# Retention and two feed-forward layers on one core: when weight preparations are split, when the first plain tile starts, and when the last activated values are stored

## The chip, the cores and the metric

The kernel runs on one core of one Trainium2 chip. The metric is the device time of one execution in microseconds. The core's engines are named as in the profile: PE (matrix products; PEld is its weight load), DVE (vector engine), ACT (scalar engine), POOL (GpSimd) and SP, which here only issues transfers. ACT issues transfers too; such a row is marked ACTq, one of SP is marked SPq. Each engine carries out its own instructions in order.

## What is computed

Four batches of eight heads go through a linear retention over 768 positions; the result, 3072 rows of 512, goes through two feed-forward layers of width 2048.

```python
state = gamma * state + k[t] outer v[t];  y[t] = scale * q[t] @ state     # per batch and head
x = y as 3072 x 512
h = x @ w_in;  g = maximum(0.01 * h, h);              x = g @ w_out       # first layer
h = x @ w_in2; g = h * (1 / (1 + exp(-1.702 * h)));   out = g @ w_out2    # second layer
```

The weights come as 64-bit floats. The chip makes 32-bit floats of them by integer steps on their two words.

## The kernel before

**Products.** Every operand of a product in the feed-forward layers is split into a rounded part ("hi", a copy on ACT) and the rest ("lo", a subtraction on DVE); three products of the parts stand for one. `split` (L153 and L150) is this pair of instructions.

**Phases.** First comes the retention in 24 steps of 128 positions (`retention`), and among its steps the 16 tiles of the first layer's `x @ w_in` for the first 512 rows. Then come the other five blocks of 512 rows, 16 tiles each (`ffn_in`): 12 matmuls of 128x512 into one of six PSUM banks, one activation on ACT that evicts it (L243), and one store that ACT issues (L245). These are the "plain" tiles. The three products that follow, first `w_out` (`Second`), second `w_in` (`First`), second `w_out` (`Second` again), use a scheme of seven block products in place of eight, for which the weights' blocks are also added and subtracted. `First` works on 32 pairs of a row block and an eighth of the width.

**Conversions in the retention.** The 16 weight tiles of the plain product are loaded (`load_raw`), converted (`convert`: two steps on ACT, L171 and L172, four on DVE, L175 to L181, then `round_up`, L190) and split (`finish`, its lo part on POOL). `W0 = 4` sets the step at which the first plain tile stands; `work` is called from two steps earlier on. A step has the scores of the next position block (L278, and their masking on DVE, L281), the state update (L317 on DVE), the output products, and the scaling of the output on DVE (`put`, L330 or L342). The scores have one place in PSUM: those of step s+2 wait until L281 has read those of step s+1.

**Preparations.** 36 half slots of later weights are prepared beside the plain tiles of blocks 1 to 5, and 12 more in the third phase. `Prep.start` gives out the steps by a clock, `Later`, that ticks once per tile: load at once; at tick 3 `words` (L171, L172 on ACT, L175 to L181 on DVE) and `sums` (L190 and three L150 on DVE); for the first 6 preparations (they are kept in place) and the first 6 of the second `w_in` (numbers 16 to 21; they are stored in two parts) also at tick 3 a split of 896 columns; at tick 4 the store. A preparation is begun whenever `given < (n + 1) * 36 // 67` for tile n. Raw words and result have three places each; the split's hi part goes back to the place of the raw words.

**The end.** The last product is written by `last_result`, twice, for 128 of the output's columns each time: two copies of PSUM, one on ACT and one on DVE, a transpose on PE, two copies again, two stores.

## Time and profile before

| | |
|---|---|
| median of 3 runs | 1090.22 us (1087.55 to 1092.33) |
| the profiled execution's own time | 1088.18 us |
| its span, first to last instruction | 1086.1 us |
| PE busy | 1057.2 us, 97% |
| DVE busy | 814.3 us, 75% |
| ACT busy | 586.7 us, 54% |
| mean granted clock of PE | 0.995 |

PE is busy nearly throughout. The page cuts the span into 40 slices of 27 us: PE reads 9 tenths or more in 37 of them, 7 in the first, and 8 in that from 272 to 299 us and in the last. The granted clock reads 9 tenths or more in each. So the places where PE waits, or where its clock fell, have to be looked for one by one, in the views of waits, windows and timelines.

### The profile page before, as it was taken

The page shows a single profiled execution, that of the slowest core. Times are in us where ns is not written, and L with a number is a line of the kernel's source. Part 1 is how long each engine was busy: PE and PEld are TensorE (multiplying, and loading weights), DVE is VectorE, ACT ScalarE, POOL GpSimd, SP SyncE. Part 2 cuts the span into 40 slices and gives each one's busy share as a digit, 9 for nine tenths or more (in the row PEclk, how much of TensorE's full clock was granted, in tenths as well). Part 3 has the DMA queues.
Part 4 walks back from the last instruction along what each step waited for, and adds up shares of the span by engine and source line. Part 5 has one row for each costly group of instructions (what it writes and reads, how often), then busy time and mean ns, then how long its engine had stood idle before and what let it go on. Part 6 is the DMA issues. An engine that isn't in the chain of part 4 may idle for free.

```text
span 1086.1 us, 16941 instructions
## 1 busy us (share of the span) xinstructions
PE 1057.2 (97%) x6042; PEld 903.9 (83%) x6043; DVE 814.3 (75%) x1384; ACT 586.7 (54%) x1114; POOL 90.3 (8%) x88
## 2 busy tenths in 40 slices
PE   7999999999899999999999999999999999999998
PEld 5777887787678888888888999999999788888886
DVE  5987736786679598688789677686767996885883
ACT  5766534554455564544545666465565645555553
POOL 1211100000000000000000203444300000000000
PEclk9999999999899999999999999999999999999999
DMA  9899664797799613723529844858387535235322
GB/s 345 304 364 395 205 214 151 250 366 260 255 330 314 207 41 100 259 76 123 190 69 320 309 145 164 289 174 283 138 281 244 218 97 190 101 97 194 105 70 78
DMA packets 128164, 225.81 MB, mean 208 GB/s; under 512 B 11088, under 2 KB 72784, under 8 KB 124752
## 3 DMA queue, kind: packets, MB, share of 16 engines
q1 hardware_dynamic: 97440, 178.29, 48.0%
q10 hardware_dynamic: 30640, 46.45, 11.7%
q8 instruction: 47, 0.77, 0.3%
q14 instruction: 37, 0.30, 0.1%
HBM read 138.71 MB, written 85.98 MB: 207 GB/s over the span
## 4 chain that ended last, share of the span: by engine, by line
PE 74%; DVE 9%; DMA 7%; ACT 4%; issue 3%; POOL 1%; ACTq 1%; SPq 0%; DVEq 0%; POOLq 0%
PE psum L758 42%; PE psum L576 18%; PE psum L239 7%; DMA gd<-e 2%; PE psum L278 2%; ACT e L243 2%; DMA b<-w1o 1%; PE psum L308 1%; DVE b L150 1%; DVE b L181 1%; DVE b L190 1%; PE psum L982 1%; DMA c<-w1i 1%; DMA h<-qkv 1%; PE psum L301 1%
## 5 line engine op out<-in xcount | busy, mean ns | idle before, releaser
L758 PE MATMUL psum<-c,h 128*128 128x512 f32 x1008 | 228.8, 389 | 0.0
L758 PEld LDWEIGHTS psum<-c,h 128*128 128x128 f32 x1008 | 189.3, 188 | 39.2
L758 PE MATMUL psum<-e,h 128*128 128x512 f32 x768 | 182.0, 391 | 1.7 <-DVE e L150 1.7
L758 PEld LDWEIGHTS psum<-e,h 128*128 128x128 f32 x768 | 143.4, 188 | 31.9 <-DVE e L150 2.5
L239 PE MATMUL psum<-d,h 128*128 128x512 f32 x576 | 139.4, 398 | 8.4 <-ACT e L243 4.9
L239 PEld LDWEIGHTS psum<-d,h 128*128 128x128 f32 x576 | 107.5, 190 | 36.0 <-ACT e L243 6.9
L239 PE MATMUL psum<-a,h 128*128 128x512 f32 x576 | 133.6, 393 | 3.3 <-ACT e L243 3.1
L239 PEld LDWEIGHTS psum<-a,h 128*128 128x128 f32 x576 | 109.0, 190 | 27.4 <-ACT e L243 3.9
L576 PE MATMUL psum<-b,h 128*128 128x384 f32 x576 | 111.0, 335 | 2.0 <-ACT psum L642 2.0
L576 PE MATMUL psum<-c,h 128*128 128x384 f32 x576 | 110.2, 334 | 0.3 <-DVE d L607 0.3
L576 PEld LDWEIGHTS psum<-b,h 128*128 128x128 f32 x576 | 100.5, 188 | 3.8 <-ACT psum L642 3.5
L576 PEld LDWEIGHTS psum<-c,h 128*128 128x128 f32 x576 | 100.6, 188 | 0.9 <-DVE d L607 0.6
L715 ACT CAST c<-b 128x512 fp32r<-128x512 f32 x96 | 59.3, 622 | 57.1 <-DVE c L150 35.6
L150 DVE TENSOR_TENSOR c<-b,c 128x512 fp32r<-128x512 f32 x96 | 65.4, 689 | 18.8 <-ACT c L715 16.6
L590 ACT ACTIVATE d<-psum 128x384 f32<-128x384 f32 x96 | 47.1, 491 | 57.3 <-PE psum L576 48.9
L715 ACT CAST e<-a 128x512 fp32r<-128x512 f32 x77 | 47.2, 622 | 43.5 <-PE psum L758 15.0
L243 ACT ACTIVATE e<-psum 128x512 f32<-128x512 f32 x80 | 47.5, 593 | 42.4 <-PE psum L239 34.2
L150 DVE TENSOR_TENSOR e<-a,e 128x512 fp32r<-128x512 f32 x77 | 52.3, 688 | 22.1 <-ACT e L715 20.9
L150 DVE TENSOR_TENSOR h<-h 128x384 fp32r<-128x384 f32 (+2 forms) x80 | 44.7, 593 | 20.6 <-ACT h L153 11.5
L150 POOL TENSOR_TENSOR a<-a 128x768 f32<-128x768 f32 x7 | 13.2, 1892 | 485.8 <-DMA h<-wds 470.7
L594 DVE TENSOR_TENSOR d<-psum,d 128x384 f32<-128x384 f32 x96 | 51.2, 548 | 2.6 <-ACT d L590 2.1
L758 PE MATMUL psum<-f,h 128*128 128x512 f32 x192 | 49.0, 390 | 0.0
(139 smaller groups left out, 1464.6 us busy)
## 6 DMA issues: line engine op xcount, KB each, us to landing
gd<-d ACTq DMA_DIRECT2D x128, 192.0 KB, 2.7
h<-qkv SPq DMA_DIRECT2D x21, 1024.0 KB, 8.0
gd<-e ACTq DMA_DIRECT2D x80, 256.0 KB, 4.7
d<-gd SPq DMA_DIRECT2D x64, 256.0 KB, 4.1
b<-gd SPq DMA_DIRECT2D x64, 256.0 KB, 3.9
a<-gd SPq DMA_DIRECT2D x48, 256.0 KB, 4.6
c<-w1i SPq DMA_DIRECT2D x16, 512.0 KB, 8.1
xd<-e SPq DMA_DIRECT2D x12, 512.0 KB, 3.2
```

Of the source, the lines that this page charges most:

```text
L150: e.tensor_tensor(out=o, in0=x, in1=y, op=ALU.subtract)
L181: lambda f, high: nc.vector.scalar_tensor_tensor(out=f, in0=f, scalar=0x7FFFFFFF, in1=high, op0=ALU.bitwise_and, op1=ALU.bitwise_or))
L190: e.tensor_tensor(out=f.bitcast(I32), in0=f.bitcast(I32), in1=low.bitcast(I32), op=ALU.add)
L239: nc.tensor.matmul(out=h, lhsT=w[:, a, k], rhs=xs[blk % 2][k][:, c], start=(i == 0), stop=(i == 3 * NP - 1), skip_group_check=True)
L243: nc.scalar.activation(out=t, in_=h, func=AF.Lrelu)
L278: nc.tensor.matmul(out=ps[:, e, n], lhsT=kT[r, n], rhs=qT[r, n], start=True, stop=True, skip_group_check=True)
L301: nc.tensor.matmul(out=kv[r, n], lhsT=ks[:, 2 * n + e], rhs=v[:, n, r], start=(c == 0 and n == 0), stop=True, skip_group_check=True)
L576: nc.tensor.matmul(out=t, lhsT=w[:, k, a], rhs=x[:, b, k], start=(start and m == 0), stop=(m == 5), skip_group_check=True)
L590: nc.scalar.activation(out=s, in_=src, func=AF.Sigmoid, scale=1.702)
L594: nc.vector.tensor_tensor(out=dst, in0=src, in1=s, op=ALU.mult)
L715: nc.scalar.copy(out=t[:, 0], in_=self.block_of(*item))
L758: nc.tensor.matmul(out=t[:, j], lhsT=w[:, j, a], rhs=x[:, b], start=(new and q == 0 and m == 0), stop=(q == NQ - 1 and m == 2), skip_group ...
```

## The change

1. **Preparations.** The split stands at tick 4 in place of 3, the store at tick 6 in place of 4. The split's hi part has a ring of its own of two places, one of which is taken from the ring of evicted tiles: that one has six places in place of eight. Preparations are begun at a rate of 36 in 64 tiles in place of 67. In the third phase a preparation's steps begin with one empty step.
2. **Retention.** `W0` is 6 in place of 4. `work` is cut in two: load and conversion stand before the step's output products (`work_first`), the split of the tile before and the rounding after the step's outputs (`work_last`). The rounding of the first two tiles is done on POOL. The first two raw loads stand in steps 1 and 2 in place of step 0. ACT's first instruction works on another piece of memory than the one that PE's warm-up products read.
3. **Third phase's end.** Stores of activated values that come due in its last iteration are put on a list, and issued two at a time behind the first products of the last phase. That phase prepares four operands ahead in place of three.
4. **The end.** The two first copies of the last product are both on ACT; each half is transposed on its own, into another bank, and stored on its own.

```diff
-    W0 = 4
+    W0 = 6
-    def work(between=lambda: None):
-        n = done[0]
-        done[0] += 1
+    def work_first(n):
         if n + 2 < KF:
             load_raw(n + 2)
-        between()
         if n < KF:
             convert(n)
+    def work_last(n):
         if 0 < n <= KF:
             finish(n - 1)
         if n < KF:
-            round_up(*conv[n])
+            round_up(*conv[n], nc.gpsimd if n < 2 else nc.vector)
...
-        nc.scalar.copy(out=idle[:, :2], in_=idle[:, 2:4])
+        first = few.view(5, 8)
+        nc.gpsimd.memset(first, 0.0)
+        nc.scalar.copy(out=first[:, :4], in_=first[:, 4:])
...
+            n = None
+            if s >= W0 - 2 and done[0] < KF + 1 and (s <= W0 or now_in[s - 1]):
+                n = done[0]
+                done[0] += 1
+                work_first(n)
             o = a_out(s)
-            if s >= W0 - 2 and done[0] < KF + 1 and (s <= W0 or now_in[s - 1]):
-                work(lambda: a_store(s, o))
-            else:
-                a_store(s, o)
+            a_store(s, o)
+            if n is not None:
+                work_last(n)
...
-            if s == 0:
-                load_raw(0)
-                load_raw(1)
+            if s in (1, 2):
+                load_raw(s - 1)
...
-    g_ring = ring(run_of(Area("e"), 8, 2), TB)
+    g_area = Area("e")
+    g_ring = ring(run_of(g_area, 6, 2), TB)
...
-            self.hi = self.raw.bitcast(F32).rearrange("p b f t -> p (b f t)")[:, : 7 * P].rearrange("p (i f) -> p i f", i=7)
+            self.hi = next(self.rings[2])
...
-                clock.at(3, self.split if split else self.keep)
+                clock.at(4, self.split if split else self.keep)
             if not keep:
-                clock.at(4, self.store_split if split else self.store)
+                clock.at(6, self.store_split if split else self.store)
...
-            out = [lambda: words_scalar(self.f, self.low, raw[:, :, 1])]
+            out = [lambda: None, lambda: words_scalar(self.f, self.low, raw[:, :, 1])]
...
-            if given < min(N_IN1, (n + 1) * N_IN1 // 67):
+            if given < min(N_IN1, (n + 1) * N_IN1 // 64):
...
-                store = lambda t: nc.scalar.dma_start(out=self.dst[f * NQ + q][:, cols], in_=t)
+                def store(t):
+                    put = lambda: nc.scalar.dma_start(out=self.dst[f * NQ + q][:, cols], in_=t)
+                    if self.ending:
+                        self.pending.append(put)
+                    else:
+                        put()
...
+                self.ending = not now
...
-            second2.begin(later2, 0, NQ, 3, 14)
+            second2.begin(later2, 0, NQ, 4, 14)
...
     def done3(n, blk, i, q):
+        for _ in range(2):
+            if first2.pending:
+                first2.pending.pop(0)()
...
         for k in range(2):
-            copy[k](t[:, k * n : k * n + n], h[:, j, k * n : k * n + n])
-
-        def turn():
-            for b in range(4):
...
+            nc.scalar.copy(out=part(t, k), in_=part(h[:, j], k))
+
+        def turn(k):
+            for b in range(2):
...
+        for k in range(2):
+            later.at(1 + k, lambda k=k: turn(k))
+            later.at(2 + k, lambda k=k: store(k))
```

Three places show what this makes of the engines' order. In the rows, the names with a letter are areas of memory; the line numbers of the change are one or a few off those of before.

ACT in block 1, around the first preparation that is kept in place (the CAST of 128x896 is its split's hi part, L171 and L172 its words, or L172 and L173 in the change; the ACTIVATE of psum is a tile's eviction). Before:

```order
L171 ACTIVATE b<-b 128x512
L172 ACTIVATE b<-b 128x512
L153 CAST h_1599<-b 128x896
L243 ACTIVATE e<-psum 128x512
L245 DMA gd_77<-e 128x512
L243 ACTIVATE e<-psum 128x512
L245 DMA gd_77<-e 128x512
L171 ACTIVATE b<-b 128x512
```

The same place in the change:

```order
L172 ACTIVATE b<-b 128x512
L173 ACTIVATE b<-b 128x512
L242 ACTIVATE e<-psum 128x512
L244 DMA gd_77<-e 128x512
L154 CAST h_1617<-b 128x896
L242 ACTIVATE e<-psum 128x512
L244 DMA gd_77<-e 128x512
L172 ACTIVATE b<-b 128x512
```

One eviction and its store moved from behind the CAST to between the words and the CAST.

DVE in the retention, around the first conversion (the four instructions from TENSOR_SCALAR of c to SCALAR_TENSOR_TENSOR are its words, ISA its rounding, the TENSOR_TENSOR of 128x1024 the masking of the scores). Before, in steps 2 and 3:

```order
L317 TENSOR_TENSOR b<-psum,f 128x256
L330 TENSOR_TENSOR h_84<-psum,f 128x2x128
L330 TENSOR_TENSOR h_84<-psum,f 64x2x128 x2
L175 TENSOR_SCALAR c_184<-c_184 128x512
L177 TENSOR_SCALAR b<-b 128x512
L179 TENSOR_SCALAR b<-b 128x512
L181 SCALAR_TENSOR_TENSOR b<-b,c_184 128x512
L190 ISA b<-c_184,b 128x1024
L281 TENSOR_TENSOR b<-psum,b 128x1024
```

In the change, in steps 4 and 5:

```order
L280 TENSOR_TENSOR b<-psum,b 128x1024
L176 TENSOR_SCALAR c_233<-c_233 128x512
L178 TENSOR_SCALAR b<-b 128x512
L180 TENSOR_SCALAR b<-b 128x512
L182 SCALAR_TENSOR_TENSOR b<-b,c_233 128x512
L316 TENSOR_TENSOR b<-psum,f 128x256
L341 TENSOR_TENSOR h_84<-psum,f 128x2x2x128
L280 TENSOR_TENSOR b<-psum,b 128x1024
```

The words moved two steps back, and within the step from behind the state update and the output's scaling to ahead of them; the rounding is no longer on DVE here.

ACT at the end of the third phase (ACTIVATE of d from psum is that phase's activation, the CAST of 128x512 an operand of the last phase). Before:

```order
L590 ACTIVATE d<-d 128x384
L590 ACTIVATE d<-psum 128x384
L586 DMA gd_78<-d 128x384 x4
L715 CAST e<-a 128x512
L715 CAST f<-a 128x512
```

In the change:

```order
L601 ACTIVATE d<-d 128x384
L601 ACTIVATE d<-psum 128x384
L727 CAST f<-a 128x512
L592 DMA gd_78<-d 128x384 x2
L727 CAST e<-a 128x512
L592 DMA gd_78<-d 128x384 x2
```

The stores moved from ahead of the operands' casts to between them, and one more operand (e) is cast earlier, in the third phase.

## Rows read from the trace of the kernel before

**Rows 1.** The page's head and its part 1: busy time, share of the span, instructions.

```profile
span 1086.1 us, 16941 instructions
...
PE 1057.2 (97%) x6042; PEld 903.9 (83%) x6043; DVE 814.3 (75%) x1384; ACT 586.7 (54%) x1114; POOL 90.3 (8%) x88
```

**Rows 2.** Waits of PE over the whole span: us in total, times, longest us.

```profile
PE psum L278 <- DVE b L281: 4.3, 2, 3.9
...
PE psum L576 <- ACT psum L642: 2.0, 4, 0.7
...
PE psum L758 <- DVE e L150: 1.7, 1, 1.7
...
PE psum L278 <- DMA h<-qkv: 1.3, 2, 0.7
```

**Rows 3.** Waits of PE from 140 to 345 us, the plain tiles beside the preparations.

```profile
PE psum L239 <- ACT e L243: 7.5, 6, 2.9
...
PE psum L239 <- DVE d L150: 3.4, 2, 2.7
```

**Rows 4.** Windows: us, each engine's busy us (x instructions), granted clock, DMA share, GB/s.

```profile
20.00:40.00 20.00, 15.18 (x193) 12.11 (x190) 16.80 (x27) 13.13 (x32) 5.24 (x4) 0.91 0.75 292
...
80.00:100.00 20.00, 19.36 (x283) 15.54 (x283) 15.43 (x26) 11.71 (x32) 2.96 (x3) 1.00 1.02 398
...
280.00:300.00 20.00, 17.59 (x69) 14.08 (x70) 13.55 (x27) 9.01 (x16) 0.00 (x0) 0.91 0.75 250
```

**Rows 5.** Timeline of PE: start, us, line, shapes, count, [idle before <- releaser].

```profile
198.04 30.24 PE L239 MATMUL psum<-d,h 128*128 128x512 f32 x132 [1.78 <-ACT e L243]
...
272.47 4.61 PE L239 MATMUL psum<-a,h 128*128 128x512 f32 x12 [2.86 <-ACT e L243]
...
281.85 5.30 PE L239 MATMUL psum<-d,h 128*128 128x512 f32 x15 [2.74 <-DVE d L150]
```

**Rows 6.** Timeline of ACT around the split of a preparation that is kept.

```profile
152.30 0.66 ACT L171 ACTIVATE b<-b 128x512 f32<-128x512 f32 x1 [0.46 <-ACT e L243]
...
156.91 0.95 ACT L153 CAST h<-b 128x896 fp32r<-128x896 f32 x1 [3.38 <-DVE b L150]
...
157.76 0.60 ACT L243 ACTIVATE e<-psum 128x512 f32<-128x512 f32 x1
...
159.76 0.67 ACT L171 ACTIVATE b<-b 128x512 f32<-128x512 f32 x1 [0.40 <-DMA b<-w1o]
```

**Rows 7.** Timeline in the retention, steps 2 to 4, PE, DVE and POOL.

```profile
16.25 1.16 PE L278 MATMUL psum<-h 64*128 64x128 f32 x16
...
19.55 1.16 PE L278 MATMUL psum<-h 64*128 64x128 f32 x16
...
21.56 1.29 POOL L150 TENSOR_TENSOR d<-h,d 128x512 fp32r<-128x512 f32 x1 [1.90 <-ACT d L339]
...
22.12 1.02 DVE L175 TENSOR_SCALAR c<-c 128x512 uint32<-128x512 uint32 x1 [1.28 <-ACT b L171]
...
25.41 1.22 DVE L281 TENSOR_TENSOR b<-psum,b 128x1024 f32<-128x1024 f32 x1
...
26.68 1.51 PE L278 MATMUL psum<-h 64*128 64x128 f32 x16 [3.87 <-DVE b L281]
```

**Rows 8.** Timeline of the start, PE and ACT.

```profile
2.78 3.60 PE L369 MATMUL psum<-f 128*128 128x512 bf16 x8 [2.78 <-ACT f L363]
...
6.20 2.02 ACT L289 ACTIVATE h<-h,f 128x64 f32<-128x64 f32 x8 [3.47 <-DMA h<-qkv]
```

**Rows 9.** Timeline where the third phase ends and the last one begins.

```profile
840.64 2.69 ACTq L586 DMA_DIRECT2D gd<-d  x4
...
844.76 1.66 PE L758 MATMUL psum<-e,h 128*128 128x512 f32 x6 [1.70 <-DVE e L150]
```

**Rows 10.** Timeline of the end, PE.

```profile
1081.69 0.66 PE L1011 MATMUL psum<-g,c 128*128 128x128 f32 x4 [0.92 <-DVE c L1005]
```

**Rows 11.** DMA issues: out<-in, queue, count, KB each, median us to landing.

```profile
wd1o<-b SPq DMA_DIRECT2D x7, 448.0 KB, 4.8
```

More of the change, by code (lines that the diff above doesn't have):

```diff
@@ L523, in __init__ @@
             self.n_banks = {k: 0 for k in p_banks}
+            self.pending = []
         def bank(self, k, w):
@@ L849, in retention_two_ffn @@
     places = [(pa, 0), (pa, 8), (pb, 0)]
-    prep_rings = ring(places, 4, P, 2), ring([(t, at + 4) for t, at in places], 8, P)
+    prep_rings = ring(places, 4, P, 2), ring([(t, at + 4) for t, at in places], 8, P), ring([(Area("f"), 0), (g_area, 12)], 7, P)
     N_IN1 = 36
@@ L1004, in last_result, with store @@
         n = TB // 2
-        copy = (lambda o, x: nc.scalar.copy(out=o, in_=x), lambda o, x: nc.vector.tensor_copy(out=o, in_=x))
+        e = second2.p_banks["e"]
+        y = out[second2.rows(blk, 0)].rearrange("(b p) f -> p b f", p=P)[:, :, j * P : j * P + P]
+        part = lambda a, k: a[:, k * n : k * n + n]
         for k in range(2):
-            copy[k](t[:, k * n : k * n + n], h[:, j, k * n : k * n + n])
-        def turn():
-            for b in range(4):
-                nc.tensor.matmul(out=h[:, j, b * P : b * P + P], lhsT=t[:, b * P : b * P + P], rhs=ident,
+            nc.scalar.copy(out=part(t, k), in_=part(h[:, j], k))
+        def turn(k):
+            for b in range(2):
+                nc.tensor.matmul(out=banks[:, e[k], b * P : b * P + P], lhsT=part(t, k)[:, b * P : b * P + P], rhs=ident,
                                  is_transpose=True, start=(b == 0), stop=True, skip_group_check=True)
-        def store():
-            y = out[second2.rows(blk, 0)].rearrange("(b p) f -> p b f", p=P)[:, :, j * P : j * P + P]
-            for k, e in enumerate((nc.scalar, nc.sync)):
-                copy[k](s[:, k * n : k * n + n], h[:, j, k * n : k * n + n])
-                e.dma_start(out=y[:, 2 * k : 2 * k + 2], in_=s[:, k * n : k * n + n].rearrange("p (b f) -> p b f", f=P))
-        later.at(1, turn)
-        later.at(2, store)
+        def store(k):
+            if k == 0:
+                nc.vector.tensor_copy(out=part(s, k), in_=banks[:, e[k], :n])
+            else:
+                nc.scalar.copy(out=part(s, k), in_=banks[:, e[k], :n])
+            (nc.sync, nc.scalar)[k].dma_start(out=y[:, 2 * k : 2 * k + 2], in_=part(s, k).rearrange("p (b f) -> p b f", f=P))
+        for k in range(2):
+            later.at(1 + k, lambda k=k: turn(k))
+            later.at(2 + k, lambda k=k: store(k))
     second2.run(later, result2, done3, {"ops": ring(run_of(tail_a[0], 4, 4) + run_of(tail_a[1], 4, 4), 2, T2),
```

## The prediction

> **What bounds the kernel now.** I read the page's busy times first: PE works 1057.2 of 1086.1 us [rows 1], so the matrix engine sets the time and some 29 us at most are to be had from its idle time. Then PE's waits, for the whole span and for the stretch of the plain tiles [rows 2, 3]: what stands there is evictions that came late (7.5 us) and operands of the next row block that came late (3.4), the masking of scores in the retention (4.3), transfers of q, k, v (1.3), the third phase (2.0), and the first operands of the last phase (1.7). Then the windows, for the clock [rows 4]: it averages 0.91 in 20 to 40 us and in 280 to 300 us. With levels of 1.2 and 2.4 GHz that is 18% of 20 us, 3.6 us, at the lower one, and half of that, 1.8 us, lost. The timeline shows the same from the matmuls: 132 at full speed take 30.24 us, 0.229 each, so a tile of 12 takes 2.75; after a wait of 2.86 us 12 took 4.61, and after one of 2.74 us 15 took 5.30 in place of 3.44, 1.86 lost each time [rows 5]. After the wait of 1.78 us nothing was lost.
>
> **Part 1, preparations.** What the reader is to see in [rows 6] is ACT standing still: words at 152.30, then 3.38 us of waiting for DVE to finish words and sums, the split's cast at 156.91, and only then two evictions at 157.76, a microsecond each with the issue of their stores, and the next words at 159.76. One preparation costs ACT 7.46 us with two evictions in it. PE makes a tile in 2.75 us, and 67/36 = 1.86 tiles pass per preparation, 5.12 us. With 1.86 evictions the round is 7.32, so ACT falls back 2.2 us per preparation, 13.2 over six. The four casts of the next row block's operands in the same block come on top; I count them at the half microsecond by which a cast of this kind delays ACT here, as an estimate from the 0.95 us of the cast that is almost twice as long [rows 6]: 2 us, in all 15.2. PE goes on through that as long as one of six banks is free, that is five tiles or 13.75 us. The overhang of 1.5 us stands beside the wait of 1.78 us that the trace has near 198 us [rows 5], so I trust the count. In the second group of six, whose hi parts also hold the raw places, most of the rest of [rows 3] arises in the same way; late operands there are DVE's subtractions, queued behind the same sums.
>
> In the change one eviction stands between words and cast, so a microsecond of the 3.38 us is used: a round takes 6.46 us with two evictions, 6.24 with the 64/36 = 1.78 of the new rate, and 4.89 us pass meanwhile. ACT falls back 1.35 us per preparation, 8.1 over six, 10.1 with the four casts: under 13.75. So the first group should stall PE no more. The second starts with a rest of lag, since DVE needs some 3.9 us (words at 152.30 to cast at 156.91, less 0.66 of ACT) of every 4.89 even without a split, and has four subtractions for the next operands in the same block: there I keep a remainder. At stake is 7.5 + 3.4 = 10.9 us of waits and two times 1.86 of slow clock, 14.6 together. I keep 2.0 of it as waiting (bounds 0 and 8, half of the stake, rounded up) and take **12.6** (6.6 to 14.6).
>
> Two things are added. Words of preparation k+3 write where the result of k lay, whose store now starts at tick 6; with 1.78 tiles per preparation they come 3 x 1.78 + 3 = 8.3 ticks after k began, 2.3 ticks or 6.4 us after the store's issue. Its median to landing is 4.8 us [rows 11]: covered, by 1.6. The hi part's two places come round 1.56 ticks, 4.3 us, after the store; a wait of half a microsecond there falls on ACT in unlagged rounds only and is inside the remainder. In return raw places come free at the sums, not when a store has landed. The smaller ring of evicted tiles comes round after six tiles, 16.5 us at PE's pace and 6 us when ACT catches up at one per microsecond: above 4.8. The empty step in the third phase moves a preparation's conversion one tick back; nothing of PE waits for it, and I count 0, with the 2.0 us of all waits there [rows 2] as bound to either side.
>
> **Part 2, retention.** A step without a tile takes PE 3.30 us (16.25 to 19.55) [rows 7]. DVE's conversion of five instructions, begun at 22.12, lets the masking of the scores start only at 25.41, though PE had made them by 20.7: PE waits 3.87 us and then runs slowly, 1.51 us in place of 1.16 for the same 16 matmuls. At stake are the 4.3 us of [rows 2] and 1.8 of clock, 6.1. In the change two conversions still stand in steps without a tile, 4 and 5. They come behind the masking, but ahead of the state update, which the next step's products need. Rounding has left DVE, so each is four fifths of 3.29 us, 2.6. PE can therefore wait up to 2 x 2.6 = 5.2; it does not, as its own scores and output products fill part of it: about 1.3 us in one step, and 0.6 after the first tile, and I add 1.0 for the two conversions' slower instructions beside POOL. I take 2.9, near the middle, so a gain of **3.2** (0.9 to 6.1). No single wait is expected above 2 us, so I count no slow clock.
>
> POOL has a part in that. In [rows 7] the TENSOR_SCALAR at 22.12 lasts 1.02 us while POOL works from 21.56 to 22.85; its end lies 0.29 us after POOL's. The Trainium skill, "SBUF — State Buffer", section "SBUF: two separate sides", says that DVE and GpSimd share a port pair as an exclusive lock for a whole instruction; the trace agrees with it here. By that rule the two roundings moved to POOL would give back up to 1.3 us each where DVE is awaited; by the row alone I have 1.0 in the sum.
>
> The warm-up products now wait for DVE's memset, not for ACT's table load, and can start some 1.5 us before 2.78; but the first scores need q and k, and ACT waited for the transfer beside them until 6.20 [rows 8]. I take **0.3** (0 to 1.5).
>
> **Part 3, third phase's end.** ACT issues four stores from 840.64 on for 2.69 us, the next operand's cast comes behind, and PE waits 1.70 us at 844.76 [rows 9]. In the change the fourth operand is ready before, and the fifth's cast comes ahead of the stores: PE has four products of 6 x 0.229 = 1.4 us to cover them. **1.7** (0.7 to 1.7).
>
> **Part 4, the end.** PE's last transposes wait 0.92 us for two copies that follow one another on ACT and DVE [rows 10]. Now the first pair needs one copy. **0.6** (0 to 0.9).
>
> **Sum.** 12.6 + 3.2 + 0.3 + 1.7 + 0.6 = 18.4. From the profiled execution's own time, 1088.2, that is 1069.8. The median of the runs lies 2.0 above that execution; with half of it I forecast **1071 us**. The ends of the terms give gains of 8 and 25.
>
> **Rivals.** (a) *Transfers bind the retention.* The share of the transfer engines is 1.02 at 398 GB/s in 80 to 100 us and 0.75 only around the stall that is to go [rows 4]; 1.3 us of PE's waits are for q, k, v already [rows 2]. For it: the queue is full. Against it: by the code's shapes a step with a tile moves 1 MB of q, k, v, half of one of weights and two quarters of results in 3.30 + 2.75 = 6.05 us, some 330 GB/s. If it holds, the 3.2 + 0.3 are lost: 1074.5. (b) *ACT still falls more than five tiles behind* in the second group, since its four operand casts and the store of hi parts meet there. For it: my count's margin is 3.7 us in the first group, and DVE is late when the second begins. It gives the 8 us of the upper bound in place of 2: 1077. (c) *POOL's lock*, the rule above: two roundings and two split subtractions of 1.3 us hold DVE in steps 4 to 6, 5.2 us in place of the 2.9 I took: 1073.3. (d) *Slower: words wait for the later store.* If stores take not 4.8 us to land but more than the 6.4 us until the words, ACT stands in about 24 preparations with evictions queued behind. ACT's rounds there need 1.2 us for the words (7.46 less wait, cast and two evictions) and 1.8 for evictions, 3.0 of 4.89, so what a wait has beyond 1.9 us adds up: with stores landing at 10.3 us, a wait of 3.9, it is 24 x 2.0 = 48 less 13.75 of cover, 34 us of new waits in place of the old 14.6: 1088.2 - 5.8 - 14.6 + 34 + 1 = 1103. Slower than before from a landing of about 9.8 us on (21 us of new waits). Against it: 4.8 us is a median of transfers in the same stretch. (e) *The split doesn't get off ACT's path*, since ACT catches up with one eviction a microsecond and then waits as before: then 1.0 us of 3.38 is all that it gains per round, which is what I counted; if the lag eats that too, part 1 is worth nothing: 1088.2 - 5.8 + 1 = 1083.4.
>
> **How the numbers follow.** Forecast 0.58; (a) 0.14; (b) 0.13; (c) 0.06; (e) 0.05; (d) 0.04. A measurement of this kernel can tell about 0.5% from no change, 5.5 us: faster is below 1084.8, slower above 1095.7. The forecast, (a), (b), (c) and a part of (e) are faster, 0.93; within 0.5% are the rest of (e) and a mild (d), 0.04; slower is (d) where it is strong, 0.03. For 8 in 10 the range goes down to the largest gain, 25 us, with the same 1 us: 1064. Upward it takes in (a), (c) and (b) and 2 us for the spread of the runs: 1079. What is left out is (d), (e) and the corners.
>
> **What would show each step.** Part 1: the wait of ACT's cast for DVE falls from 3.4 to about 2.4 us where ACT lags, PE's waits from 140 to 345 us fall from 10.9 to 2, the clock reads 1.00 in every window there. Part 2: no wait above 2 us at the masking, the plain blocks begin 3 us earlier. Part 3: no wait at the last phase's first products. Part 4: two transposes begin right after one copy. I am wrong if ACT's words wait for stores, if PE's waits for q, k, v grow beyond 3 us, or if evictions still end PE's waits by the half dozen.

## The result, and the profile after

The changed kernel takes **1073.55 us** (median of 4 runs, 1071.55 to 1075.39) where the kernel before takes 1090.73 (1087.55 to 1092.33): a ratio of 0.985, 95% interval 0.982 to 0.987. That is 17.2 us less. The forecast was 1071, with a range of 1064 to 1079. The profiled execution of the changed kernel took 1073.59 us.

The page's head and PE's busy time, to stand beside [rows 1]:

```profile
span 1071.5 us, 16963 instructions
...
PE 1052.3 (98%) x6042; PEld 902.4 (84%) x6043; DVE 816.0 (76%) x1380; ACT 585.4 (55%) x1116; POOL 93.3 (9%) x91
```

The span is 14.6 us shorter. (The other 2.6 of the 17.2 between the medians are in no trace: the profiled execution of before, at 1088.18, lay 2.5 us below the median of its runs, that of after at its own.) Waits of PE over the whole span, to stand beside [rows 2]; the same code has another line number in the changed file, so L281 of before is L280 now, L239 is L238, L150 is L151, L317 is L316, L642 is L654 and L758 is L770:

```profile
PE psum L238 <- DVE d L151: 3.3, 1, 3.3
PE psum L277 <- DMA h<-qkv: 3.2, 4, 1.5
PE psum L581 <- ACT psum L654: 2.1, 2, 1.5
PE psum L300 <- DVE b L316: 2.0, 2, 1.8
PE psum L238 <- ACT e L242: 1.6, 2, 1.3
...
PE psum L770 <- DVE e L151: 1.0, 2, 0.5
...
PE psum L277 <- DVE b L280: 0.2, 1, 0.2
```

The masking's 4.3 us (L281) are down to 0.2; of the 8 us of late evictions 1.6 are left; of the late operands (`d`, L151) 3.3 are left as one wait. New are waits for the state update (L300 behind L316, 2.0), more of them for q, k, v (3.2 in place of 1.3), and one of 1.5 in the third phase, where the four waits of 2.0 in all have become two of 2.1.

To see where the gain lies I cut each trace at PE's own landmarks: the first product behind the retention's last output, the first products of the second, third and last phase, the end of the last phase's products, and the end of the span. The time from the first landmark to the second is called the plain blocks'. A kernel of the experiments below ran them without one wait of PE, in 217.7 us; what a kernel has beyond that is called its **stall**.

| us | before | after | gain | forecast |
|---|---|---|---|---|
| start and retention, to | 137.14 | 134.05 | 3.1 | 3.2 + 0.3 |
| plain blocks | 234.7 (stall 17.0) | 225.4 (stall 7.7) | 9.3 | 12.6 |
| second phase | 228.9 | 228.9 | 0 | 0 |
| third phase | 238.0 | 236.8 | 1.1 | 0 |
| last phase | 242.0 | 241.6 | 0.4 | 1.7 |
| behind the last product | 5.3 | 4.7 | 0.6 | 0.6 |

What is left in the plain blocks stands at one place, in PE's timeline, to be read beside [rows 5]:

```profile
254.77 10.42 PE L238 MATMUL psum<-a,h 128*128 128x512 f32 x44
266.53 2.34 PE L238 MATMUL psum<-d,h 128*128 128x512 f32 x9 [1.33 <-ACT e L242]
272.18 10.76 PE L238 MATMUL psum<-d,h 128*128 128x512 f32 x39 [3.31 <-DVE d L151]
283.17 32.93 PE L238 MATMUL psum<-d,h 128*128 128x512 f32 x144 [0.23 <-ACT e L242]
```

Behind two waits 39 matmuls took 10.76 us where 39 x 0.229 is 8.93: 1.8 us more, at a slower clock. The windows say the same, beside [rows 4]: a granted clock of 0.91 from 260 to 280 us, and of 1.00 from 20 to 40, where it had been 0.91.

```profile
20.00:40.00 20.00, 17.45 (x291) 14.37 (x289) 19.12 (x30) 16.77 (x46) 7.85 (x6) 1.00 0.93 346
260.00:280.00 20.00, 15.36 (x59) 11.78 (x58) 14.77 (x30) 9.50 (x16) 0.00 (x0) 0.91 0.65 223
```

Why ACT and DVE are late there is read from their queues. ACT's timeline, beside [rows 6]:

```profile
153.66 0.94 ACT L154 CAST h<-b 128x896 fp32r<-128x896 f32 x1 [2.35 <-DVE b L151]
...
160.17 0.95 ACT L154 CAST h<-b 128x896 fp32r<-128x896 f32 x1 [2.89 <-DVE b L151]
...
226.28 0.66 ACT L172 ACTIVATE c<-c 128x512 f32<-128x512 f32 x1 [8.00 <-DMA b<-w1o]
...
264.52 0.94 ACT L154 CAST f<-c 128x896 fp32r<-128x896 f32 x1 [2.38 <-DVE c L151]
```

A round from one cast to the next, with two evictions in it, takes 6.5 us (153.66 to 160.17) where it took 7.5 before (156.91 to 164.39). The listed wait of the cast fell by less, from 3.4 to 2.9 us in four of the twelve rounds, to 2.4 in five (four of these have an operand's cast ahead as well) and to between 3.3 and 3.7 in three: this view counts the issue of the eviction's store as idle. But at 226.28 a preparation's words held ACT for 8.0 us on a transfer, three tiles long, just before the second group of splits begins. SP's queue in that time (load of raw words L423, operands of the block after next L205, store of a finished preparation L443):

```profile
211.81 0.99 SPq L423 DMA_DIRECT2D c<-w1o  x2
218.53 0.34 SPq L205 DMA_DIRECT2D c<-xd  x1
218.92 0.43 SPq L443 DMA_DIRECT2D wd1o<-c  x1
219.40 1.58 SPq L423 DMA_DIRECT2D b<-w1o  x2
```

SP stood from 212.8 to 218.5, because L205 may only be issued when DVE has made the last subtraction from the old operands (it ended at 218.5). The store of result `c`, whose data were ready at 212.9, stood behind it, and with it the place that the words at 226.28 write. (The row names a load issued at 219.40 as what the words waited for; the store landed 7.3 us after 218.92, at 226.2, as well.) From 264.6 to 272.2 SP stood again, the store of the next result `c` was issued at 273.01 and landed 8.4 us later, and the words that write there waited for 6.2 us until 281.40.

### The profile page after: what moved, and what is told of

Same layout as the page of the kernel before. It is cut to its first block, busy times and chain, and to the rows that moved or that the text cites. A ratio compares the mean times of both kernels' runs of the same rounds, so it can differ in the third digit from the quotient of the medians.

```text
span 1071.5 us, 16963 instructions
## 1 busy us (share of the span) xinstructions
PE 1052.3 (98%) x6042; PEld 902.4 (84%) x6043; DVE 816.0 (76%) x1380; ACT 585.4 (55%) x1116; POOL 93.3 (9%) x91
## 4 chain that ended last, share of the span: by engine, by line
PE 78%; DVE 8%; DMA 8%; ACT 3%; issue 2%; ACTq 0%; SPq 0%; DVEq 0%
PE psum L770 40%; PE psum L581 21%; PE psum L238 12%; DMA h<-qkv 2%; PE psum L277 1%; DMA b<-w1o 1%; PE psum L307 1%; DMA b<-gd 1%; DVE b L151 1%; PE psum L994 1%; DMA wd1o<-b 1%; DVE b L191 1%; DMA xd<-h 1%; PE psum L300 1%; DMA gd<-e 1%
## 5 line engine op out<-in xcount | busy, mean ns | idle before, releaser
L770 PE MATMUL psum<-c,h 128*128 128x512 f32 x1008 | 228.8, 389 | 0.0
L770 PEld LDWEIGHTS psum<-c,h 128*128 128x128 f32 x1008 | 189.2, 188 | 39.3
L770 PE MATMUL psum<-e,h 128*128 128x512 f32 x768 | 182.1, 391 | 1.0 <-DVE e L151 1.0
L770 PEld LDWEIGHTS psum<-e,h 128*128 128x128 f32 x768 | 143.3, 188 | 31.6 <-DVE e L151 1.3
L238 PE MATMUL psum<-d,h 128*128 128x512 f32 x576 | 138.2, 397 | 4.9 <-DVE d L151 3.3
L238 PEld LDWEIGHTS psum<-d,h 128*128 128x128 f32 x576 | 107.8, 190 | 31.1 <-DVE d L151 3.7
L238 PE MATMUL psum<-a,h 128*128 128x512 f32 x576 | 131.5, 389 | 0.0
L238 PEld LDWEIGHTS psum<-a,h 128*128 128x128 f32 x576 | 107.9, 188 | 23.0 <-ACT e L242 0.4
L151 DVE TENSOR_TENSOR c<-b,c 128x512 fp32r<-128x512 f32 x96 | 65.4, 689 | 18.8 <-ACT c L727 16.6
L151 DVE TENSOR_TENSOR h<-h 128x384 fp32r<-128x384 f32 (+2 forms) x80 | 44.9, 595 | 31.9 <-ACT h L154 20.4
L151 DVE TENSOR_TENSOR e<-a,e 128x512 fp32r<-128x512 f32 x77 | 52.3, 688 | 18.5 <-ACT e L727 17.1
L151 POOL TENSOR_TENSOR a<-a 128x768 f32<-128x768 f32 x7 | 13.2, 1891 | 509.4 <-DMA h<-wds 461.4
L770 PE MATMUL psum<-f,h 128*128 128x512 f32 x192 | 49.0, 390 | 0.0
```

Of the source, the lines that this page charges most:

```text
L151: e.tensor_tensor(out=o, in0=x, in1=y, op=ALU.subtract)
L238: nc.tensor.matmul(out=h, lhsT=w[:, a, k], rhs=xs[blk % 2][k][:, c], start=(i == 0), stop=(i == 3 * NP - 1), skip_group_check=True)
L770: nc.tensor.matmul(out=t[:, j], lhsT=w[:, j, a], rhs=x[:, b], start=(new and q == 0 and m == 0), stop=(q == NQ - 1 and m == 2), skip_group ...
```

## The experiments

Each kernel is the changed one with the edit shown, except where "before" is said. Times are medians of 4 or more runs, ratios are against the kernel before on the same chip; the columns behind them, in us, come from one trace of each kernel. "Pace 67" means that 36 preparations are begun over 67 tiles in place of 64.

| kernel | us | ratio, 95% | retention to | stall | third | last |
|---|---|---|---|---|---|---|
| changed | 1073.6 | 0.982 to 0.987 | 134.1 | 7.7 | 236.8 | 241.6 |
| split at tick 3 | 1090.8 | 1.000 to 1.002 | 135.5 | 22.9 | 237.6 | 241.5 |
| before, split at tick 4 | 1075.0 | 0.985 to 0.989 | 138.9 | 2.6 | 238.0 | 241.6 |
| hi part in the raw place | 1076.1 | 0.986 to 0.990 | 133.3 | 9.0 | 238.1 | 242.5 |
| operands split 4 tiles earlier | 1072.5 | 0.982 to 0.987 | 133.2 | 7.0 | 237.1 | 241.0 |
| pace 67 | 1068.2 | 0.979 to 0.982 | 133.4 | 1.8 | 237.8 | 241.1 |
| operands' transfer 6 tiles later | 1074.2 | 0.982 to 0.988 | 137.2 | 3.7 | 237.3 | 242.5 |
| pace 67, transfer later | 1067.7 | 0.978 to 0.982 | 134.7 | 0.0 | 237.0 | 241.5 |
| first tile early, new order | 1085.3 | 0.996 to 0.998 | 147.0 | 6.8 | 236.6 | 241.7 |
| first tile late, old order | 1071.8 | 0.982 to 0.985 | 132.7 | 8.1 | 236.5 | 242.3 |
| pace 67, transfer later, roundings on DVE | 1067.8 | 0.978 to 0.983 | 135.3 | 0.0 | 237.8 | 240.9 |
| stores in front | 1075.8 | 0.986 to 0.989 | 134.4 | 8.2 | 236.9 | 241.2 |
| no empty step | 1076.1 | 0.985 to 0.989 | 137.9 | 7.6 | 239.2 | 241.8 |

The retention's end scatters by 4.7 us between the nine kernels with the same retention (133.2 to 137.9), with the waits for q, k, v; so questions on the plain blocks are decided by the stall and not by the whole time. The stall scatters less: the five kernels whose plain blocks are the same (changed, first tile early, first tile late, stores in front, no empty step) have 6.8 to 8.2, so a difference of less than about 1.4 us shows nothing by itself. The last phase, the same in eleven kernels (all but the kernel before, its variant and "stores in front"), takes 240.9 to 242.5.

### The split's place

```diff
-                clock.at(4, self.split if split else self.keep)
+                clock.at(3, self.split if split else self.keep)
```

> The changed kernel with one thing undone: the preparations' split stands at tick 3 again, right behind its sums; its own ring, the later store and the new rate stay. Theory A (the gain of the plain stretch comes from the eviction that now stands between words and split): ACT's round is 7.24 us against 4.89 us per preparation again, 2.35 us of lag each, 14.1 over six and 2 for the operands' casts, over the 13.75 us of cover; PE's waits in the plain stretch go from 4.9 back to 10 us or more, the time from 1073.5 to 1081 to 1085. Theory B (the gain comes from raw places that come free at the sums and from SP, no longer held up by stores): at most 2 us are lost, 1075.5 or less.

The whole gain was gone, more than either theory asked for. PE's waits from 140 to 345 us:

```profile
PE psum L238 <- ACT e L242: 10.5, 7, 2.8
PE psum L238 <- DVE d L151: 3.2, 2, 2.6
PE psum L238 <- DVE a L151: 1.0, 1, 1.0
```

The evictions' waits are back, and larger than in [rows 3], and the cast waits 3.4 us again in eleven of twelve rounds. So the split's place is worth the whole gain of part 1 and more, and something else in part 1 costs about 6 us (a stall of 22.9 where the kernel before has 17.0). The other direction, the kernel before with this one number changed (and the store behind the split, which stood there already):

```diff
 (before)
-                clock.at(3, self.split if split else self.keep)
+                clock.at(4, self.split if split else self.keep)
```

> The kernel before with one number changed: the split of a preparation one tile behind its sums (tick 4), its store with it; the hi part stays in the raw place, the old pace of 67, the old retention and end. Theory A: the split's place is nearly the whole of part 1 and the rest of that part (own places for hi, stores at tick 6, pace 64) gives nothing or costs: plain blocks 219.5 to 222 us (234.7 before), time 1074 to 1077 (13 to 16 below the kernel before). Theory B: without the hi part's own places the raw loads come late and the gain is the 9.3 us of the changed kernel or less: 225 to 230 us and 1080 to 1085.

Theory A. One number gives a stall of 2.6 in place of 17.0, and 13.7 us of the time on its chip (1075.0 against 1088.7). PE's waits from 140 to 345 us, which were 10.9 in [rows 3]:

```profile
PE psum L239 <- ACT e L243: 1.2, 1, 1.2
PE psum L239 <- DVE a L150: 0.8, 1, 0.8
```

### The hi part's own places and the later stores

```diff
-    g_ring = ring(run_of(g_area, 6, 2), TB)
+    g_ring = ring(run_of(g_area, 8, 2), TB)
...
-            self.hi = next(self.rings[2])
+            self.hi = self.raw.bitcast(F32).rearrange("p b f t -> p (b f t)")[:, : 7 * P].rearrange("p (i f) -> p i f", i=7)
...
-                clock.at(6, self.store_split if split else self.store)
+                clock.at(4, self.store_split if split else self.store)
```

> The changed kernel with the hi part of the split back in the raw words' place, the ring of evicted tiles back at eight places, and the store back at tick 4; the split stays at tick 4. Theory A (one eviction between words and split is what gains): 0 to 2 us slower than the changed kernel, 1073.5 to 1075.5. Theory B (raw places and stores are what gains): raw loads wait for stores again, most of the 9.3 us of the plain stretch is lost, 1080 to 1083.

A stall of 9.0 in place of 7.7, so Theory A: these edits are worth some 1 us, which the scatter of the stall does not let one tell from nothing. The time, at 1076.1, is 2.5 us longer and just outside Theory A's 1075.5; the third and last phase have 2.1 of that, and the edit does not touch them.

### The pace, and what stands in SP's queue

```diff
-            if given < min(N_IN1, (n + 1) * N_IN1 // 64):
+            if given < min(N_IN1, (n + 1) * N_IN1 // 67):
```

> The changed kernel with the old pace of the preparations (36 in 67 tiles in place of 64); the split stays one tile behind. Theory A: what is left of the plain blocks' idle time (4.9 us of waits and 1.8 of slow clock near 272 us) is ACT's and DVE's lag in the second group, and it shrinks with the pace: 5.12 us pass per preparation in place of 4.89, so ACT falls back 1.2 us in place of 1.35 and DVE gains 0.2 per preparation; the plain blocks come to 221 to 224 us (225.4 in the changed kernel), the time to 1068 to 1072. Theory B: the pace is worth nothing by itself, since what is late meets at one place, the next block's four subtractions between preparations: 225 to 227, the time within 2 us of the changed kernel's 1073.6. Against A would be a time above 1075: then the denser pace is what keeps the preparations clear of something that comes later.

The time fell by another 5 us (4 by the ratios), as in Theory A, and the plain blocks took 219.6 us, less than its 221 to 224. Six kernels make three pairs for the pace, and the stall is about 6 us larger with 64 in each: split at 3, 17.0 (before) to 22.9; split at 4 with the old places, 2.6 to 9.0; with the new places, 1.8 to 7.7. Only the last pair differs in nothing else (the second also in the retention and the ends, the first in the hi part's places and the store as well). The pace also changes the tiles beside which each preparation's steps stand; no run separates that from the denser work. What is left at 67 is one wait. ACT's and SP's timelines there:

```profile
263.74 0.94 ACT L154 CAST f<-c 128x896 fp32r<-128x896 f32 x1 [2.39 <-DVE c L151]
...
272.41 0.94 ACT L154 CAST e<-b 128x896 fp32r<-128x896 f32 x1 [6.10 <-DMA wds<-e]
```

```profile
255.59 1.22 SPq L420 DMA_DIRECT2D b<-w2i  x2
264.34 0.33 SPq L205 DMA_DIRECT2D c<-xd  x1
264.72 0.42 SPq L455 DMA_DIRECT2D wds<-e  x1
```

The cast waits 6.1 us for its place `e`; the store that empties it was issued at 264.72, behind L205, though its data were ready near 257.6 (the cast that fills it ended then). Two more kernels ask whether that transfer is the cause. One moves it alone, at pace 64:

```diff
-            x_load(q + 1)
+            later.at(6, lambda: x_load(q + 1))
```

> The changed kernel (pace 64, split at tick 4), with one thing moved: the transfer of the block after next's operands (1 MB, issued on SP behind the last operand subtraction of a block) is issued six tiles later. In the changed kernel SP stands at that transfer until DVE has made the subtraction (211.8 to 218.5 us, and 263.4 to 272.2), the store of a finished preparation stands behind it (218.9 in place of some 213), and ACT's words wait 8.0 us until 226.28 for the place that this store empties, so that the second group begins with a lag of three tiles. Theory C: that is the cause of what is left of the plain blocks' idle time; the wait of 8 us falls to under 3, the waits of 4.9 us and the slow clock near 272 us go, the plain blocks come to 219.5 to 221.5 us (225.4 in the changed kernel), the time to 1067 to 1070. Theory A': it is the pace of 64 alone, DVE and ACT being too slow for 4.89 us per preparation whatever SP does: 224 to 226 us and 1072 to 1074.

Between 217 and 275 us the longest wait of words is 2.5 us in place of 8.0 (one of 6.0 stands earlier, at 205.71, and PE does not feel it), no eviction is late any more, and the stall is 3.7 in place of 7.7. One wait for the operands' subtraction stays; PE's timeline:

```profile
273.47 41.82 PE L238 MATMUL psum<-d,h 128*128 128x512 f32 x183 [3.34 <-DVE d L151]
```

So SP's queue is 4.0 of the 7.7, and Theory C holds for these. The time, 1074.2 where Theory C has 1067 to 1070, did not follow, since in this kernel's trace the retention ended at 137.2 and the last phase took 0.9 more: by the time alone it would have been no gain. The last 3.7 go with the pace:

> The changed kernel with both: the old pace of 67 and the operands' transfer issued six tiles later. With the pace alone one wait of 1.5 us for an eviction was left at 272 us, behind a cast that waited 6.1 us for the hi part's place, whose store SP issued at 264.72 behind that transfer. Theory C: this wait goes too, and the plain blocks run at 80 tiles x 2.74 = 219.2 us or within 0.4 of it (219.56 with the pace alone), the time is 1066 to 1068.5. Theory A': the 1.5 us stay or move, 219.6 to 221 us and 1068 to 1070.

Theory C. With both edits the view of PE's waits from 140 to 345 us is empty, and the granted clock is 1.00 in the window that had 0.91:

```profile
260.00:280.00 20.00, 20.00 (x90) 16.57 (x89) 16.80 (x35) 11.85 (x20) 0.00 (x0) 1.00 0.82 297
```

This kernel, 1067.7 us (0.980, 0.978 to 0.982), is the fastest of the study; the pace alone (1068.2) cannot be told from it by its time, only by the stall. Alone the pace takes 5.9 off the stall and the later transfer 4.0, together 7.7: the two overlap.

### The next operands' split

```diff
-                if m in (8, 9, 10, 11):
-                    x_split(blk + 1, m - 8)
+                if m in (4, 5, 6, 7):
+                    x_split(blk + 1, m - 4)
```

> The changed kernel with the next row block's operands split beside tiles 4 to 7 of each block in place of 8 to 11. Theory A (the wait of 3.3 us for the last of these operands at 272 us, and the slow clock behind it, arise since they are queued behind three split preparations four tiles ahead of their use): with eight tiles ahead both go, 3.3 + 1.8 = 5.1 us, 1068.4. Theory B (DVE and ACT are behind by the same work wherever it stands, so evictions are late in place of operands): the wait moves to evictions, at most 2 us faster, 1071.5 or more.

Theory B. The operands were in time, and an eviction was 3.3 us late in their stead:

```profile
PE psum L238 <- ACT e L242: 4.3, 3, 3.3
```

The stall, 7.0, lies in the scatter around 7.7: the lag only changes the place where PE meets it.

### The retention

The first tile early again, with the new order in the step and the roundings on POOL kept:

```diff
-    W0 = 6
+    W0 = 4
...
-            if s in (1, 2):
-                load_raw(s - 1)
+            if s == 0:
+                load_raw(0)
+                load_raw(1)
```

> The changed kernel with the first plain tile at step 4 again and both first raw loads in step 0; words ahead of the state update and the first roundings on POOL stay. Theory A (two steps later is what gains, as the conversions then meet steps whose masking and scaling are shorter on DVE): a wait of 2 to 4 us at steps 2 to 4 comes back with its slow clock, 3 us slower than the changed kernel, 1076.5. Theory B (the order within the step is what gains): 0 to 1 us slower. Theory C (fewer transfers waits, 3.2 us in the changed kernel at steps 5, 6 and later, since tiles give them time): 1 to 2 us faster.

The retention ended 13 us later than in the changed kernel and 10 later than before, where the most that a theory gave was 3. PE and DVE around the first of four such waits:

```profile
23.52 0.69 PE L300 MATMUL psum<-h 128*64 128x64 f32 x16 [3.11 <-DVE b L316]
```

```profile
21.09 0.43 DVE L176 TENSOR_SCALAR c<-c 128x512 uint32<-128x512 uint32 x1 [2.47 <-ACT b L172]
...
22.96 0.42 DVE L316 TENSOR_TENSOR b<-psum,f 128x256 f32<-128x256 f32 x1
```

DVE's queue had the conversion at its head, waiting 2.47 us for ACT, and the state update (L316) behind it. ACT had scaled the keys of a later step (L288, 17.92 to 19.93) and then waited 0.47 us for the raw words, so that its own part of the words began at 20.40. In the changed kernel the step of the first conversion has no such scaling just ahead of it, and ACT began the words at 24.22, right behind the cast of 23.70. The new order puts words ahead of the state update; it is affordable only where ACT comes to the words in time. The old order with the late tile:

```diff
-                work_first(n)
             o = a_out(s)
             a_store(s, o)
             if n is not None:
+                work_first(n)
                 work_last(n)
```

> The changed kernel with the later first tile and GpSimd's rounding kept, but the conversion of a step put back behind the step's outputs and state update. It completes the run with the early tile and the new order, where the retention ended at 147.0 us. Theory A (as predicted: two conversions still stand in steps that have no tile, and behind the outputs they hold the next masking): the wait of near 4 us at the masking comes back once or twice, the retention ends at 136 to 138 (134.05 in the changed kernel, 137.14 before), the time 1075 to 1078. Theory B: the later start and the rounding on GpSimd are the whole gain and the order is indifferent: 133.5 to 134.5 and 1073 to 1074.

Theory B, and a little beyond it: the retention ended at 132.7, with 0.2 us of waits for the masking, where the two kernels with the old retention have 4.3 and 4.0. DVE's timeline at the first conversion has no idle time ahead of it:

```profile
25.56 0.69 DVE L341 TENSOR_TENSOR h<-psum,f 128x512 f32<-128x512 f32 x1 [0.40 <-PE psum L313]
26.17 0.42 DVE L176 TENSOR_SCALAR c<-c 128x512 uint32<-128x512 uint32 x1
```

So the later first tile, with the later raw loads that go with it, takes the masking's wait away, and the new order adds nothing to that. At last the roundings, in the fastest kernel:

```diff
-            round_up(*conv[n], nc.gpsimd if n < 2 else nc.vector)
+            round_up(*conv[n])
```

> The last kernel (pace 67, operands' transfer six tiles later; 1067.7 us, retention to 134.7, plain blocks without a wait), with the rounding of the first two tiles back on DVE. In the changed kernel the two roundings on GpSimd (27.61 and 32.57 us, 1.29 and 1.31 us) lie beside DVE operations that read PSUM and take their usual 0.68 and 1.21 us; the three that were held (1.02, 1.68 and 1.40 in place of 0.42, 0.69 and 0.43) lie beside the split's subtractions, which this kernel keeps. Theory A: the roundings cost DVE nothing on GpSimd and save it 2 x 0.69 us, so on DVE they cost 0 to 1.4: retention to 134 to 136, time 1067 to 1069. Theory B (the rival of the shared port): DVE was held for the roundings too, so that bringing them back gains 1 us or more: retention to 132 to 133.5, time 1065 to 1067, and fewer waits of the outputs for DVE. In both, the three held operations stay.

Theory A. No difference (1067.8 against 1067.7, retention 0.6 later, far inside its scatter): the roundings on POOL neither cost nor bring anything that can be measured.

### The third phase and its end

```diff
-                    if self.ending:
+                    if False:
                         self.pending.append(put)
```

> The changed kernel with the third phase's last stores back in their old place, ahead of the fifth operand's cast on ACT; four operands are still ready before. Theory A: the issue of the four stores (2.69 us on ACT) is what the last phase's first products waited for, and four products of 1.4 us cover half of it: a wait of 0.8 to 1.3 us on ACT's cast near 846 us, last phase 242.2 to 242.8 us (241.6 in the changed kernel, 242.0 before). Theory B: DVE's subtraction for the operands, which now shows two waits of 0.5 us there, is the limit, and the stores' place is worth under 0.3 us: 241.4 to 241.9. Time 1073 to 1075 in both.

Theory B, though the time of 1075.8 lies above its 1075. With the stores back in front, the last phase took 241.2 us, and the only wait of its products is one for a subtraction:

```profile
856.08 4.42 PE L770 MATMUL psum<-e,h 128*128 128x512 f32 x18 [0.49 <-DVE e L151]
```

So the stores' place is worth nothing that can be seen beside a fourth operand ready. That this operand alone removed the 1.70 us of [rows 9] follows from it only by exclusion; three operands with late stores were not run.

```diff
-            out = [lambda: None, lambda: words_scalar(self.f, self.low, raw[:, :, 1])]
+            out = [lambda: words_scalar(self.f, self.low, raw[:, :, 1])]
```

> The changed kernel without the empty step ahead of a preparation's words in the third phase. Theory A: that step is where the third phase's 1.1 us came from (237.96 us before, 236.83 after), since the conversion no longer stands ahead of the eviction on ACT: without it 237.7 to 238.3 us and the wait of 1.5 us at 795 us goes to another place. Theory B: the empty step moves nothing that PE waits for and the 1.1 us come from elsewhere (other kernels of this study had 236.6 to 238.1 there without touching it): within 0.5 us of 236.8, or anywhere in that scatter, with the waits of the third phase in the same number. Time 1073 to 1075.

Theory A, and beyond its 238.3. The third phase took 239.2 us, above all eleven changed kernels with the empty step (236.5 to 238.1, mean 237.2), and five short waits stand where [rows 2] has four; the one of 1.5 us at 795 us is gone:

```profile
PE psum L581 <- ACT psum L654: 2.7, 5, 0.7
```

The empty step is worth 1 to 2 us (238.0 in both kernels of before, 239.2 here, against 237.2). That follows the number of the waits and not their sum, which is 2.0 before, 2.1 with the empty step and 2.7 here; what each costs beyond the listed idle time stays open.

## Why the prediction was right, and where its terms were off

**Part 1** (12.6 forecast, 6.6 to 14.6; 9.3 measured). The mechanism was right: an eviction between words and cast, ACT's round down from 7.5 to 6.5 us (6.46 in the count), the first group without a wait. But 9.3 is a sum of three terms of which I had sized one, and that it lies in the range is partly luck.

The split's place brings 14 to 15 (17.0 to 2.6 at pace 67; 22.9 to 7.7 at 64), the hi part's places and later stores some 1, if anything, and the pace of 64 takes 6 of it back. The step that failed is the remainder, "I keep 2.0 of it as waiting": it was 7.7, all in the second group, where rival (b) had put its 8. (The gain is 9.3 and not the rival's 6.6 because the stake was 17.0 and not 14.6: the listed waits and the two losses of the clock leave 2.4 out, in stretches such as the 24 matmuls of 5.74 us at 190.52 in the kernel before, where 24 x 0.2285 is 5.48.)

I had put the pace into the count as 4.89 us in place of 5.12 per preparation, 0.2 us each, and there it is small. As far as the runs show, its cost is where the lag meets other work: at the end of a block, DVE's subtractions of the next operands come later, SP stands at L205 until they are done, stores stand behind SP, and words or casts behind the stores. "Covered, by 1.6" was the sentence that missed it, in both its terms. These stores took not 4.8 us from issue to landing but 6.8 and 6.0 (medians of the seven and three to `wd1o` in the changed kernel), so 6.4 us of cover were about used up. And I took the store's issue at its tick; that of `c` came some 6 us later, on a queue whose order I had not read past. That is the mechanism of rival (d), words that wait for a store, where PE feels it at one preparation in a block instead of 24: 4.0 us by the run that moved the transfer. The other 3.7 us go with the pace; how it makes them, beyond the lag, stays open.

ACT's words waiting for stores was also one of the three signs by which I wanted to see myself wrong, and the waits for q, k, v beyond 3 us were another: two of the three appeared, with the time inside the range.

**Part 2** (3.2 and 0.3 forecast, 3.1 measured together). In sum right: nine kernels with the new retention end it at 134.9 us on average, two with the old one at 138.0 (137.1 and 138.9). The two ranges touch, since two of the nine end at 137.2 and 137.9, so the size of 3.1 is not firm; that the masking's wait of 4 us is gone is. Its working was partly wrong. Of two conversions "in steps without a tile" I expected 2.9 us of waits; the state update (L300) waits 2.0 us, and the transfers of q, k, v 3.2 in place of 1.3. That looks like a weak form of rival (a), PE coming earlier and finding q, k, v late, but it is not shown: the same retention has 1.0 to 4.1 us of these waits in nine kernels, the old one 1.3 and 1.5 in two. The start brought 0.6 in place of 0.3: the scores issued in step 2 begin at 15.66 where [rows 7] has 16.25.

**Rival (c), the shared port.** The held instructions are there, but not beside the roundings. POOL and DVE in the changed kernel:

```profile
24.39 1.28 POOL L151 TENSOR_TENSOR d<-h,d 128x512 fp32r<-128x512 f32 x1 [2.15 <-ACT d L338]
27.61 1.29 POOL L191 TENSOR_TENSOR b<-b,c 128x512 int32<-128x512 int32 x1 [1.94 <-ACT h L288]
30.67 1.27 POOL L151 TENSOR_TENSOR h<-b,h 128x512 fp32r<-128x512 f32 x1 [1.77 <-ACT h L154]
```

```profile
24.94 1.02 DVE L176 TENSOR_SCALAR c<-c 128x512 uint32<-128x512 uint32 x1
...
27.73 0.68 DVE L341 TENSOR_TENSOR h<-psum,f 128x512 f32<-128x512 f32 x1
28.32 1.21 DVE L280 TENSOR_TENSOR b<-psum,b 128x1024 f32<-128x1024 f32 x1
...
30.81 1.68 DVE L182 SCALAR_TENSOR_TENSOR b<-b,c 128x512 uint32<-128x512 uint32 x1
```

Beside the rounding at 27.61 DVE read PSUM and took its usual 0.68 and 1.21 us; beside the split's subtractions it worked on SBUF alone and took 1.02 for 0.43, 1.68 for 0.69, each ending 0.3 to 0.6 us behind POOL. (The later tiles' subtractions on POOL go on holding one such instruction each, 1.66 us in place of 0.69 at 40.89 and 1.47 in place of 0.43 at 45.92.) The Trainium skill, "SBUF — State Buffer", section "SBUF: two separate sides", limits the lock to vector instructions in a two-port mode or with two SBUF inputs; the rows agree with that limit, which I had left out when I priced the roundings at a full 1.3 us each.

**Part 3** (1.7 forecast, 0.4 measured). The wait of 1.70 us, 6 us into the last phase, is gone; two new ones of 0.5 for DVE's subtractions, 21 and 30 us into it, took 1.0 of it back:

```profile
846.62 5.68 PE L770 MATMUL psum<-e,h 128*128 128x512 f32 x24 [0.49 <-DVE e L151]
...
855.56 4.38 PE L770 MATMUL psum<-e,h 128*128 128x512 f32 x18 [0.53 <-DVE e L151]
```

I had asked what covers the cast on ACT, and not who is next: the subtraction behind it. A net gain is not shown: eleven kernels with the new end take 240.9 to 242.5 us for the last phase, the two with the old one 242.0 and 241.6.

**The third phase** (0 forecast, within 2.0; 1.1 measured) was my "nothing of PE waits for it". The kernel without the empty step has five waits of PE for ACT's evictions (L654) in place of two, and the longer phase: PE does wait for what stands behind the conversion on ACT.

**Part 4** was right: PE's last transposes wait 0.46 us in place of 0.92, and the time behind the last product fell by 0.6.

The sum came within 2.6 us partly by luck. Terms that were too large (part 1 by 3.3, part 3 by 1.3, part 2 with the start by 0.4) stood beside one that I had put at 0 (the third phase, 1.1), so that the gain was 3.9 too large; and the 1 us that I had added for the spread of the runs, which the changed kernel's median over its profiled execution does not show, hid about 1 of that.

## What to carry to other kernels

When an engine's queue holds a step and its successor, put work of another stream between them, and change only that first: here one number gave a ratio of 0.987 (13.7 us) and the whole change 0.985, since one of its other edits cost 6 us of what the rest brought. When a pace is raised or a store is moved, read the queue that issues it to its end: a transfer that waits for a late engine holds every store behind it, and the price is paid by whoever needs the places. And when terms of a few us are to be told apart, cut the trace into stages, since the whole time carries the scatter of the others.

## What the runs showed of the hardware

- **Equal retentions, unequal ends.** With the same code for it the retention ended between 133.2 and 137.9 us, with 1.0 to 4.1 us of waits for q, k, v. That is more than most single edits here are worth.
- **A wait of 3.3 us need not cost the clock.** After 3.31 us of waiting at 272.18 in the changed kernel 39 matmuls lost 1.8 us; it had waited 1.33 us at 266.53, some 6 us before. After 3.34 us at 273.47 in the kernel with the later transfer 183 matmuls took 41.82 us, 0.2285 each: nothing lost, and the view lists no other wait of PE from 140 to 345 us. Shorter waits cost it elsewhere: [rows 5] has losses of 1.86 after 2.86 and 2.74, and in the kernel with the split at tick 3 a wait of 2.05 at 187.73 was followed by 24 matmuls in 7.38 us where 5.48 is usual. What decides it stays open.
